# Attention then experts on one core: row numbers in their own tile, the experts' memory in another order, and the factor table made head pair by head pair

## The chip, the cores and the metric

The kernel runs on one core of one Trainium2 chip. The metric is the device time of one execution in microseconds (us). The engines are TensorE (PE; its weight loads are shown as PEld), VectorE (DVE), ScalarE (ACT), GpSimd (POOL) and the sync engine (SP), whose queue issues nearly all plain transfers. Each engine runs its own instructions in order; semaphores tie the engines to each other and to the transfers.

## What is computed

Two blocks in a row, all in float32. The first is attention with a sliding window and a bias that falls with distance; the second is a mixture of experts in which each token goes to the one expert that its logits choose, and none is dropped.

```python
# attention: batch 8, heads 8, sequence 576, head dim 64
scores = q @ k.T / sqrt(64)
rel    = pos[:, None] - pos[None, :]
slopes = 2.0 ** (-8.0 * (arange(8) + 1) / 8)            # one per head
scores = where((rel >= 0) & (rel < 128), scores - slopes * abs(rel), -1e9)
x      = softmax(scores) @ v                            # to (4608 tokens, 512)

# experts: 8 of them, hidden size 1024
logits = x @ w_gate                                     # (4608, 8)
e      = argmax(logits, axis=1)
gate   = softmax(logits)[e]
out[t] = gate[t] * (relu(x[t] @ w1[e[t]]) @ w2[e[t]])
```

## The kernel before

**Attention.** The work is cut into 32 units: 8 batches by 4 pairs of heads. A unit has four steps, written out by hand in one loop (`for u in range(NU + 1)`). `scores(u)` multiplies k by q on TensorE into four PSUM banks `sp` and takes the exponential on ScalarE into two tiles `e`. `factors(u, s)` multiplies `e` by a table `fac` on VectorE, L564 and L569. The table holds exp(-slope x distance) for each head, and zero outside the window, so bias and mask cost one product. `merge(u)` adds halves that belong to the same query on GpSimd, into `mg` (L576, L579). `values(u - 1, ...)` multiplies by v, and `totals(u - 1)` sums the weights with a matmul by a column of ones (L614), both on TensorE and one unit behind. The loads of q and k (`load_qk`, L534 and L535) run four units ahead, in a pool of five buffers.

**The table.** It is made once, ahead of the first unit. GpSimd writes a constant for each tile that is needed later (an identity, a triangle, counters, a row of zeros), then a matrix of distances `rel`. VectorE multiplies it by the eight slopes (L500), GpSimd cuts the window out with two selects over all heads (L501, L505), ScalarE takes the exponential over all heads (L509), and VectorE copies parts of it into the layout that the second half of a unit reads (L510 to L512). All of `scores(0)`'s exponentials stand behind L509 on ScalarE, and `factors(0, 0)` stands behind the copies, further small constants and `start_routing()` on VectorE.

**Routing.** As soon as a batch's attention is done, a list of tasks turns it into logits, chooses the expert, and sends each token's row to a DRAM buffer `x_rows`, sorted by expert, with an indirect transfer from GpSimd's queue (`scatter`, L178). A row is 514 words: 512 of x, then the token's number (as an integer), then its gate. The loop takes a few tasks from the list at two places in each unit (`do(n)`): none in the first seven units, and more in the last batch than in others. Eight transfers (`clear_rows`, L112) set `x_rows` to zero early on.

**The first two tiles of expert 0.** When all but the last two batches are routed, two tiles of 128 rows of expert 0 are complete. `early_group()` loads them, and `last_tasks()` does their transposes and layers among the tasks of the last batch. Their results are scaled by the gate into a tile `e` of attention's pool `ex`, and `send_out` (L416) sends each row to its place in the output, with an indirect transfer that takes its row numbers from an SBUF tile.

**The experts.** `experts(True)` runs 15 groups: the rest of expert 0 (two tiles), then by turns a small group x of one tile (rows that did not fit into an expert's 512) and a full expert of four tiles. A full expert uses a seven-product scheme in place of eight (`seven1`, `seven2`, matmuls at L880), a small group plain products (`layer1`, L450, and `layer2`, L458). At the head of each group's turn the kernel issues the *next* group's row load, `gather` (L981), into one of two buffers `xg`, then its w2. After the group's first layer comes w1 of the group after next, and the next group's rows are transposed on TensorE (`turn`, L441). Two facts about `xg` matter:

- Next to x it holds each row's token number and gate. ScalarE's scalings (L950, L462) read the gate; `send_out` reads the token number in place, through `ids_of_rows`. Only small groups copy theirs to a tile `si` first (`tokens`, with a mask that hides rows of others).
- With two buffers, the load issued during a small group goes into the buffer of the full expert just ahead of it, whose last sends have only just gone out.

**Memory.** Tile pools are stacked. Attention's pools close before the experts' open, so both start at the same base, and a tile of the experts has to wait for whatever attention kept at the same addresses. Attention opens, in this order and with these sizes per partition: `tab` (table, 17.0 KB), `ld` (q, k, v, 42.5 KB), `ex` (probs, e, mg, 31 KB), then the pools of x and routing. The experts' `moe_pools()` opens `weights1` (32 KB), `moe_sums` (32 KB), `moe_x` (the two `xg`, 16.1 KB), then two more. A second pool of weights, `weights0`, stays open throughout.

## Time and profile before

The median of three runs is 787.58 us (785.68 to 787.88); the profiled execution spans 785.5 us.

| engine | busy us | share of the span | instructions |
|---|---|---|---|
| TensorE, matmuls | 720.9 | 92% | 4646 |
| TensorE, weight loads | 585.1 | 74% | 4646 |
| VectorE | 367.8 | 47% | 618 |
| ScalarE | 225.8 | 29% | 535 |
| GpSimd | 175.1 | 22% | 186 |

Busy time of TensorE by stage, from the windows of the trace:

| stretch, us | what runs | TensorE busy | granted clock | GB/s of all transfers |
|---|---|---|---|---|
| 0 to 20 | table, first unit | 10.73 of 20 | 0.83 | 337 |
| 20 to 40 | units 2 to 5 | 17.91 of 20 | 1.00 | 325 |
| 120 to 200 | units with routing | 74.38 of 80 | 1.00 | 194 |
| 200 to 280 | last units, early group, first group | 68.59 of 80 | 0.91 | 104 |
| 350 to 380 | an expert, a small group, the next expert's rows | 27.12 of 30 | 0.94 | 198 |
| 380 to 400 | inside a full expert | 20.00 of 20 | 1.00 | 148 |

The trace puts an idle stretch of an engine down to whatever released the instruction after it: "PE tp L441 <- DMA xg<-x_rows" is time in which TensorE stood before a transpose at L441 until a row load had landed. A chain of waits follows the work that ended last back to the start, step by step. The granted clock is the share of TensorE's full speed that its throttle allowed in that stretch.

### The profile page before, as it was taken

What the parts mean: (1) busy time and instruction counts of PE and PEld (TensorE: products, weight loads), DVE (VectorE), ACT (ScalarE), POOL (GpSimd) and SP (SyncE); (2) the same over time, 40 slices, a digit from 0 to 9 for tenths busy, and PEclk for the clock granted to TensorE, in tenths of its full rate; (3) what the DMA queues carried; (4) which work ended last, traced back from release to release, by engine and by line L of the source; (5) the groups of instructions that cost most, each with busy time, mean ns of one, the idle gap of its engine ahead of it and who ended that gap; (6) DMA issues with size and microseconds to landing.
All of it is one profiled execution on the core that took longest, in us unless ns stands there. A gap on an engine that the chain in (4) does not pass through costs nothing.

```text
span 785.5 us, 11571 instructions
## 1 busy us (share of the span) xinstructions
PE 720.9 (92%) x4646; PEld 585.1 (74%) x4646; DVE 367.8 (47%) x618; ACT 225.8 (29%) x535; POOL 175.1 (22%) x186
## 2 busy tenths in 40 slices
PE   5899999999798799998999899899989989998992
PEld 4676777777583657887789688778968877896881
DVE  4567677776853022632543264254326335332620
ACT  3554465545421112222122121212212122121210
POOL 4537565776721010002001000200200020020001
PEclk8999899999999699999999999999999999999996
DMA  9996588762211738234830832483183247214001
GB/s 337 323 381 225 167 259 288 226 215 96 82 55 41 254 121 305 100 108 160 293 107 31 304 117 107 154 298 107 41 302 111 107 164 287 108 53 166 1 0 58
DMA packets 54286, 130.72 MB, mean 166 GB/s; under 512 B 4175, under 2 KB 4175, under 8 KB 54224
## 3 DMA queue, kind: packets, MB, share of 16 engines
q1 hardware_dynamic: 47696, 110.97, 41.0%
q0 software_dynamic: 6000, 18.92, 6.4%
q8 instruction: 38, 0.62, 0.3%
q14 instruction: 24, 0.20, 0.1%
q10 hardware_dynamic: 528, 0.02, 0.0%
HBM read 102.55 MB, written 28.12 MB: 166 GB/s over the span
## 4 chain that ended last, share of the span: by engine, by line
PE 67%; issue 13%; DVE 6%; DMA 5%; POOL 4%; ACT 3%; SPq 0%; POOLq 0%; DVEq 0%
PE b L880 16%; PE a L880 11%; PE c L880 11%; PE a L458 6%; PE sp L550 5%; PE m L595 5%; DMA xg<-x_rows 4%; PE sm L614 2%; PE m L693 1%; DMA out_dram<-zo,xg 1%; PE a L450 1%; PE m L450 1%; PE tp L441 1%; DVE probs L564 1%; PE b L450 1%
## 5 line engine op out<-in xcount | busy, mean ns | idle before, releaser
L416 POOL DMA_INDIRECT out_dram<-zo,xg x28 | 29.7, 1060 | 325.6 <-ACT zo L950 321.3
L550 PE MATMUL sp<-q_sb,k_sb 64*128 64x256 f32 (+2 forms) x640 | 72.0, 368 | 9.2 <-DMA k_sb<-in_kT_dram 5.2
L557 ACT ACTIVATE e<-sp 128x512 f32<-128x512 f32 x128 | 66.4, 601 | 47.3 <-PE sp L550 43.8
L550 PEld LDWEIGHTS sp<-q_sb,k_sb 64*128 64x128 f32 x640 | 63.5, 199 | 19.9 <-DMA q_sb<-in_qT_dram 5.1
L576 POOL TENSOR_TENSOR mg<-probs 128x768 f32<-128x768 f32 x31 | 57.4, 1850 | 74.0 <-DVE probs L569 30.0
L564 DVE TENSOR_TENSOR probs<-e,fac 128x1024 f32<-128x1024 f32 x32 | 46.8, 1463 | 46.3 <-ACT e L557 30.6
L595 PE MATMUL m<-probs,v_sb 128*64 128x256 f32 (+3 forms) x768 | 63.9, 315 | 2.3 <-DVE lgw L660 1.5
L595 PEld LDWEIGHTS m<-probs,v_sb 128*64 128x64 f32 x768 | 48.6, 138 | 18.9 <-issue 4.3
L458 PE MATMUL a<-w,h 128*128 128x512 f32 x128 | 56.9, 597 | 0.0
L950 ACT ACTIVATE zo<-zo,xg 128x256 f32<-128x256 f32 x42 | 19.1, 500 | 119.1 <-DVE zo L961 77.9
L880 PE MATMUL a<-xgT,w 128*128 128x256 f32 x224 | 53.0, 379 | 0.0
L880 PE MATMUL b<-xTs,w1s 128*128 128x256 f32 x224 | 52.9, 379 | 0.0
L880 PE MATMUL a<-w,h_sb 128*128 128x256 f32 x224 | 50.6, 379 | 0.0
L880 PE MATMUL b<-w2s,hs 128*128 128x256 f32 x224 | 50.6, 379 | 0.0
L880 PEld LDWEIGHTS a<-xgT,w 128*128 128x128 f32 x224 | 42.5, 190 | 8.7 <-issue 3.3
L178 POOL DMA_INDIRECT x_rows<-xs,slots x36 | 41.2, 1143 | 26.4 <-DVE xs L696 13.3
L880 PEld LDWEIGHTS b<-xTs,w1s 128*128 128x128 f32 x224 | 42.6, 190 | 5.8
L880 PEld LDWEIGHTS b<-w2s,hs 128*128 128x128 f32 x224 | 42.6, 190 | 5.8
L880 PEld LDWEIGHTS a<-w,h_sb 128*128 128x128 f32 x224 | 42.1, 190 | 5.5
L458 PEld LDWEIGHTS a<-w,h 128*128 128x128 f32 x128 | 24.2, 194 | 27.1 <-issue 27.1
L569 DVE TENSOR_TENSOR probs<-e,fac 128x1024 f32<-128x1024 f32 x32 | 41.2, 1288 | 0.0
L441 PE MATMUL tp<-ident,xg 128*128 128x128 f32 x92 | 16.4, 329 | 23.6 <-DMA xg<-x_rows 23.6
(211 smaller groups left out, 1164.6 us busy)
## 6 DMA issues: line engine op xcount, KB each, us to landing
w<-in_moe_w_dram SPq DMA_DIRECT2D x30, 2048.0 KB
q_sb<-in_qT_dram SPq DMA_DIRECT2D x32, 288.0 KB
k_sb<-in_kT_dram SPq DMA_DIRECT2D x32, 288.0 KB
x_rows<-zero_row SPq DMA_DIRECT2D x8, 1028.0 KB
xg<-x_rows SPq DMA_DIRECT2D x16, 514.0 KB
v_sb<-in_v_dram SPq DMA_DIRECT2D x8, 1024.0 KB
v_sb<-in_v_dram SPq DMA_DIRECT2D x8, 256.0 KB
xg<-x_rows SPq DMA_DIRECT2D x7, 257.0 KB
```

The lines of the kernel that those rows point to most:

```text
L178: ins = nc.gpsimd.indirect_dma_start(out=x_d[:, :], out_offset=bass.IndirectOffsetOnAxis(ap=slots[:, t : t + 1], axis=0), in_=row, in_offs ...
L416: ins = nc.gpsimd.indirect_dma_start(out=out[:, :], out_offset=bass.IndirectOffsetOnAxis(ap=g["ids"](g, j), axis=0), in_=row, in_offset=No ...
L441: nc.tensor.transpose(tp[:, db * P : (db + 1) * P], g["xg"][:, j, db * P : (db + 1) * P], ident[:])
L450: nc.tensor.matmul(ps[:, :n], lhsT=g["w1"][:, db, fb * P : (fb + 1) * P], rhs=g["xT"][:, db, :n], start=(db == 0), stop=(db == DB - 1),)
L458: nc.tensor.matmul(ps[:], lhsT=g["h"][:, fb, j * P : (j + 1) * P], rhs=g["w2"][:, fb, :], start=(fb == 0), stop=(fb == FB - 1),)
L550: nc.tensor.matmul(sps[s][par][:, c : c + n], lhsT=k_sb[u][half, k_lo[j] : k_lo[j] + P], rhs=q_sb[u][half, q0 : q0 + n], start=True, stop= ...
L557: nc.scalar.activation(exps[u][s][:, par, :], sps[s][par][:], AF.Exp, scale=D ** -0.5)
L564: nc.vector.tensor_tensor(to.rearrange("p a (j c) -> p a j c", c=2 * P), e.rearrange("p a (j c) -> p a j c", c=2 * P), fac[:, heads, None, ...
L569: nc.vector.tensor_tensor(to, e[:], fac2[:, heads, :], op=ALU.mult)
L576: eng.tensor_add(mg[:, :, : 3 * P].rearrange("p a (t c) -> p a t c", c=P), two[:, :, :, 0, :], two[:, :, :, 1, :],)
L595: nc.tensor.matmul(xp[par * HALF : (par + 1) * HALF, lo - q0 : hi - q0], lhsT=v_sb[b][:, j, h * D : (h + 1) * D], rhs=probs[u][:, par, c + ...
L880: nc.tensor.matmul(out_of[:, i, :], lhsT=lhs(i, k), rhs=rhs(k), start=(first and i == 0 and k == 0), stop=(k == nk - 1), skip_group_check= ...
```

## The change

It has four parts.

1. **Row numbers in their own tile.** Every group now copies its token numbers to a tile `si` of its own (two buffers, in the pool `plain`), by `tokens(g)`, with the mask for small groups and a plain copy for others. `send_out` reads them from there, so that a send no longer reads `xg`.
2. **The experts' memory by when attention lets go of it.** `weights1` opens after `moe_sums` and `moe_x`. The row buffers then lie where attention kept q, k and v, and the second pool of weights lies where it kept the last v and its probabilities.
3. **The table by head pair.** All distances and selects are made per pair of heads, ahead of everything else; constants that are needed later wait in a list `later`. Only the first pair's exponential and copies are done ahead of unit 0; `table(u + 1)` follows `factors` and `merge` of units 0 to 2. `start_routing()` moves behind unit 0.
4. **Pacing.** The last batch takes as many tasks per unit as the others do: at most one and two or three.

```diff
-    make_identity(nc, ident[:])
+    later = [lambda: make_identity(nc, ident[:])]
...
+    later.append(routing_constants)
...
-            out=out[:, :], out_offset=bass.IndirectOffsetOnAxis(ap=g["ids"](g, j), axis=0),
+            out=out[:, :], out_offset=bass.IndirectOffsetOnAxis(ap=g["si"][:, j : j + 1], axis=0),
...
-    def ids_of_rows(g, j):
-        return g["xg"].bitcast(I32)[:, j, Dm : Dm + 1]
-
-    def ids_masked(g, j):
-        return g["si"][:, j : j + 1]
+    def tokens(g):
+        bits = g["xg"].bitcast(I32)[:, : g["n"], Dm]
+        si = g["si"] = plain.tile([P, NJ], I32, name="si", bufs=2)[:, : g["n"]]
+        if "mask" in g:
+            nc.vector.tensor_tensor(si, bits, g["mask"][:, 0, :], op=ALU.bitwise_and)
+            nc.vector.tensor_tensor(si, si, g["mask"][:, 1, :], op=ALU.bitwise_or)
+        else:
+            nc.vector.tensor_copy(si, bits)
...
-        for h in range(H):
-            nc.vector.tensor_scalar_mul(fac[:, h, :], rel, 2.0 ** (-8.0 * (h + 1) / H))
-        nc.gpsimd.affine_select(
-            fac, fac, compare_op=ALU.is_ge, fill=MASKED,
-            base=0, pattern=[[0, H], [1, 2 * P]], channel_multiplier=-1,
-        )
...
-        nc.scalar.activation(fac, fac, AF.Exp, scale=-1.0)
-        nc.vector.tensor_copy(fac2[:, :, 2 * P : 3 * P + HALF], fac[:, :, : P + HALF])
-        nc.vector.tensor_copy(fac2[:, :, 3 * P + HALF :], fac[:, :, HALF:P])
+        def distances(hp):
+            pair = fac[:, 2 * hp : 2 * hp + 2, :]
+            for i in range(2):
+                nc.vector.tensor_scalar_mul(pair[:, i, :], rel, 2.0 ** (-8.0 * (2 * hp + i + 1) / H))
+            nc.gpsimd.affine_select(
+                pair, pair, compare_op=ALU.is_ge, fill=MASKED,
+                base=0, pattern=[[0, 2], [1, 2 * P]], channel_multiplier=-1,
+            )
...
+        def table(hp):
+            heads = slice(2 * hp, 2 * hp + 2)
+            nc.scalar.activation(fac[:, heads, :], fac[:, heads, :], AF.Exp, scale=-1.0)
+            nc.vector.tensor_copy(fac2[:, heads, 2 * P : 3 * P + HALF], fac[:, heads, : P + HALF])
+            nc.vector.tensor_copy(fac2[HALF:, heads, 3 * P + HALF :], fac[HALF:, heads, HALF:P])
+
+        for hp in range(HP):
+            distances(hp)
+        for make in later:
+            make()
+        table(0)
...
-        start_routing()
...
-            do(0 if slow else 1 if b < NB - 1 else 2)
+            do(0 if slow else 1)
             if u < NU:
                 factors(u, 1)
                 merge(u)
+                if u + 1 < HP:
+                    table(u + 1)
+                if u == 0:
+                    start_routing()
...
-            do(0 if slow else 2 if len(tasks) < 14 and b < NB - 1 else 3)
+            do(0 if slow else 2 if len(tasks) < 14 else 3)
...
-        w_pools[1] = st.enter_context(tc.tile_pool(name="weights1", bufs=1))
         pools["s"] = st.enter_context(tc.tile_pool(name="moe_sums", bufs=1))
         pools["x"] = st.enter_context(tc.tile_pool(name="moe_x", bufs=2))
+        w_pools[1] = st.enter_context(tc.tile_pool(name="weights1", bufs=1))
...
-            if "mask" in g:
-                tokens(g)
+            tokens(g)
```

## The prediction

> **What bounds the kernel now.** I read the page first, then who waits for whom on TensorE and on the queue of the sync engine (SP), then the chain of waits in three stretches, and last the busy time by windows.
>
> The page's first part: TensorE is busy for nine tenths of the span.
>
> ```profile
> PE 720.9 (92%) x4646; PEld 585.1 (74%) x4646; DVE 367.8 (47%) x618; ACT 225.8 (29%) x535; POOL 175.1 (22%) x186
> ```
>
> Of 785.5 us, 64.6 are left in which TensorE is idle. Some 20 us of these lie outside any reach (5.1 before the first q and k land, 15 after the last matmul at 770.2). So what counts is the other 44 us, and matmuls that ran slowly. TensorE's own list of waits names most of it:
>
> ```profile
> PE tp L441 <- DMA xg<-x_rows: 23.6, 8, 7.9
> PE sm L614 <- POOL mg L579: 6.2, 4, 2.1
> PE sp L550 <- DMA k_sb<-in_kT_dram: 5.2, 1, 5.2
> PE sp L550 <- ACT e L557: 4.1, 1, 4.1
> ```
>
> The row loads xg stand first: eight waits, 23.6 us. Why are they late? The same list for SP, which issues them:
>
> ```profile
> SPq L981 <- DMA out_dram<-zo,xg: 153.0, 7, 30.0
> SPq L981 <- DMA x_rows<-xs,slots: 40.4, 1, 40.4
> SPq L981 <- DMA out_dram<-e,xg: 16.3, 2, 9.5
> ```
>
> The loads wait for the sends of the *results*: a send reads its row numbers out of xg itself, so the buffer is held until the send has landed. The chain of waits over one hand-over from an expert to the small group after it (355 to 374 us; start, length, what):
>
> ```profile
> 360.05 0.91 ACT zo L950 x2
> 362.30 2.73 DMA out_dram<-zo,xg
> 365.66 4.62 DMA xg<-x_rows
> ```
>
> ScalarE reads xg for the last time at 360.96; the send lands at 365.03; the loads go out at 365.24. TensorE has finished the small group's first layer at 366.43 and waits 2.56 us, to 368.99. The six hand-overs after full experts wait 2.56, 2.55, 2.42, 2.49, 2.32 and 2.64 = 15.0 us; the one after the first group 0.72; the one at the end of attention 7.93. Together 23.6.
>
> The chain at the end of attention:
>
> ```profile
> 252.60 2.72 DMA out_dram<-e,xg
> 255.58 3.81 DMA xg<-x_rows
> 259.53 1.95 PE tp L441 x8
> 262.41 3.75 PE a L450 x8
> ```
>
> The scatters that this load needs had landed at 238.9 (the 40.4 us wait ended there). It then stood 16.3 us more, for the two early sends out of a tile e, whose memory the xg buffer takes over. And TensorE comes back slow: 3.75 us for eight matmuls that take 1.89 later.
>
> The chain at the start:
>
> ```profile
> 6.31 1.96 POOL fac L501
> 8.32 1.96 POOL fac L505
> 10.30 1.92 ACT fac L509
> 12.24 0.96 DVE fac L510
> 17.77 2.88 POOL mg L576
> 20.64 1.41 POOL mg L579
> ```
>
> The first scores are done at 8.65, but ScalarE can't turn to them before 12.11, and VectorE's first product waits for copies until 15.34. Unit 2's scores start at 22.76; from there a unit takes 4.55 us, all of it TensorE.
>
> **What the Trainium skill says.** "TensorE: Matmul & The Clock Gate", Part 1 (what's actually happening): about 3.4 us of idling halves the clock, about 3.4 us of work restores it, in windows that run freely. The trace agrees in kind: the first hand-over below (eight transposes after 2.55 us of idling) is slow, the second isn't, so it depends on where the window lies.
>
> ```profile
> 438.26 1.97 PE L441 MATMUL tp<-ident,xg 128*128 128x128 f32 x8 [2.55 <-DMA xg<-x_rows]
> 507.05 1.09 PE L441 MATMUL tp<-ident,xg 128*128 128x128 f32 x8 [2.42 <-DMA xg<-x_rows]
> ```
>
> "DMA: Bandwidth & Descriptors", anatomy of one DMA: about 2 us of a DMA are fixed, mostly the receipt of its last byte. The send's 2.73 us fits; no queue order makes it shorter, so the gain must come from not waiting for it. "SBUF — State Buffer", who interferes with whom: a VectorE instruction with two SBUF inputs contends with GpSimd's reads. The trace agrees: mg took 2.88 us beside such products, 1.81 alone.
>
> **The change part by part.**
>
> *Row numbers in a tile si.* VectorE copies them once per group (a new copy of 2 or 4 integers; the nearest row, the masking of si, takes 0.15 us; nine copies, 1.4 us in all). For a full expert the copy stands behind the hidden sums and before a wait for TensorE of 3 to 4 us: hidden. The copy waits only for xg, and for the sends of the si two groups back, long landed. In exchange xg is free when ScalarE's last scaling ends: the load goes out at 361.1 in place of 365.24. The first part needs 3.75 us (365.24 to 368.99): 364.9. The second landed 4.62 after its issue at 365.66: 4.1 earlier, 366.2, when it is wanted after 367.5. Both are before their use, so the wait is gone whole: 15.0 us for six. The queue of SP then holds w2, which waits for TensorE's end of that expert (359.3), and w1, which waits for the small group's first layer: neither comes ahead of the rows. The slow clock goes too. From tp's start to the next layer's first matmul took 3.16, 3.42, 2.33, 3.40, 2.37 and 3.33 us; at 2.33 each, 4.0 less. I take 3.0 of these, as a cold window may fall elsewhere: **-18.0** (15 to 19.5). The first hand-over, held by a plain send: **-0.7**.
>
> *Memory.* Attention's pools stack as table 17.0 KB per partition, q/k/v to 59.5 KB, probs/e/mg to 90.5 KB. Before, the experts' order weights 32 KB, sums 32, xg 16.1 lays xg at 64 to 80 KB, over probs and e. After, sums, xg, weights: xg lies at 32 to 48 KB, over q/k/v, read for the last time at 217; the weights over the rest of these and e. So the first load waits for the scatters alone: out at 239, landed at 242.8; layer two of the early group ends on TensorE at 251.6. Gone: 7.93 of waiting, and the slow clock: tp 1.94 against 1.09, layer one 3.75 and 2.68 against 1.89 = 3.5. Against it 0.7, ScalarE's copy behind its scaling to 252.33. **-10.7** (8 to 11.4). The new wait: w1 of the first small group is held by the early sends, to 255.3. It was issued at 257.28 before, so it isn't later. Behind it on SP stand the small group's rows and w2. At 2 MB by the 380 GB/s of the start, 5.5 us, plus 2, w1 lands by 263 and the rows by 265; they are wanted at 252.3 + 1.0 + 13.9 = 267, w1 at 281. Hidden by some 2 us; the least certain margin here.
>
> *Table and start.* GpSimd begins with the distances: index and cast end near 1.6 (0.33 and 0.40, from 0.8), VectorE's eight products of 0.21 near 3.3. The two selects of 1.95 become four pairs of pieces of 1.95 / 4 = 0.49: pair 0 done near 3.2, all near 6.4; the constants (2.9 us of GpSimd before the index, 0.8 to 3.7) come after, to about 10. ScalarE's table load is 1.28; a pair's exponential is 512 wide, 0.6 like an e: done by 4.5. VectorE's copies and memsets, 3.1 us in all, shrink to about 2.2 and begin at 4.5: done by 7. So TensorE's scores, from 5.15, are now what is waited for: half done at 6.9, e from 7.0 to 9.7, products 9.8 to 11.0. Unit 1's q and k: at about 385 GB/s, 2.49 MB of queue ahead of and with them land near 9.3; scores(1) 9.3 to 12.5 (cold clock 13.5); values(0) to 14.6 (16.5); mg(0) from 11.0, 2.3 alone or 4.3 beside VectorE, to 13.3 or 15.3; totals; scores(2) between 15.2 and 17.5 in place of 22.76. Middle 16.3: **-6.5** (5 to 7.5). Three later exponentials (0.6) and six copies (about 0.3) fall in units 1 to 3, where ScalarE has 2.9 and VectorE 2.4 of 4.55 us: hidden.
>
> Do the loads follow? The windows:
>
> ```profile
> 60.00:65.00 5.00, 5.00 (x62) 3.85 (x58) 4.79 (x9) 2.86 (x6) 1.55 (x3) 1.00 0.96 347
> 65.00:70.00 5.00, 5.00 (x60) 3.49 (x60) 2.72 (x3) 3.13 (x7) 4.60 (x5) 1.00 0.41 119
> ```
>
> (busy PE, PEld, DVE, ACT, POOL; granted clock, DMA share, GB/s.) The transfers run without a pause to 65 us. Added up in queue order with the zeroing of rows: unit 5's q and k are complete at 6.16 MB, near 18.5, wanted at 29; unit 9's at 12.7 MB, near 36, wanted at 52. The margin holds.
>
> *Pacing.* Two or three tasks per unit in the last batch become at most one and two. In the new order unit 30's mg stands ahead of three scatters on GpSimd instead of behind them, which cost 2.02 us (part of the 6.2); a 1.48 us wait for the gate's product may go or move. **-2** (0 to -3).
>
> Sum: 18.0 + 0.7 + 10.7 + 6.5 + 2.0 = 37.9; 787.6 - 37.9 = 749.7.
>
> **Rivals.**
> - *Start bound by transfers* (0.08): DMA share is 1.0 from 2.5 us on. If units 1 and 2 wait for q and k, or the constants hold up mg(0), some 5.5 of the 6.5 are lost: 755. Against: unit 2's loads are at 3.08 MB, near 11.
> - *The rows stay late* (0.07): two 514 KB halves beside w2 and the last sends; a new releaser takes the place of the send, all six waits remain and only the rest comes: 787.6 - 19.9 = 768. Against: 1.5 us of slack, and the first load has little traffic beside it.
> - *Slower* (0.03): the pieces of the table enter the path of units 1 to 3 (3 x 0.9 = 2.7), the nine copies too (1.4), and a small group's rows behind the held w1 cost as much as the load before saved, so that nothing is gained: 787.6 + 4.1 = 792. For it: SP works in order. Against: ScalarE and VectorE have room, and the held load leaves earlier than before.
>
> **How the numbers follow.** The likeliest case, 0.82, is 749.7. With all lower bounds it is 787.6 - 28.7 = 759, with all upper ones 787.6 - 42.3 = 745. Both at once are unlikely; 744 to 758 holds some 0.75 of the first case and nearly all of the second: 0.8. Faster by over 0.3%: 0.96; within: 0.01; slower: 0.03.
>
> **What would show it.** Right: TensorE's waits for xg fall from 23.6 us to under 2; SP's waits at the row loads name ScalarE in place of sends; the transposes at the end of attention follow the last early matmul within 1 us; unit 2's scores begin near 16. Wrong: a new wait before these transposes, a wait for q or k in the first units, a transpose of the first small group behind its rows, or a half clock in places where it was full.

## The result, and the profile after

The changed kernel takes 748.10 us (median of four, 747.69 to 748.83) beside 786.80 us before (785.68 to 787.88): ratio 0.9509, 95% interval 0.9491 to 0.9528. The profiled executions span 785.5 and 747.0 us, and the traces' 38.5 us are what is accounted for below. The forecast was 749.7.

First part of the page, changed kernel:

```profile
PE 706.0 (95%) x4646; PEld 573.1 (77%) x4646; DVE 371.0 (50%) x633; ACT 226.1 (30%) x538; POOL 175.7 (24%) x192
```

The number of matmuls is the same, yet TensorE is busy 14.9 us less: the same matmuls ran faster, at a granted clock of 0.990 in place of 0.966. The other 23.6 us are waits.

TensorE's list of waits, changed kernel (us in all, times, longest):

```profile
PE sm L635 <- POOL mg L600: 7.8, 4, 3.5
PE a L450 <- DMA xg<-x_rows: 3.8, 5, 1.7
PE a L459 <- DVE si L439: 0.9, 1, 0.9
PE tp L450 <- ACT e L471: 0.8, 1, 0.8
```

The 23.6 us before the first transposes (tp) are gone. Four things are new: 3.8 us for the *second* half of an expert's rows (a), a wait of 0.8 us at the end of attention, a wait of 3.5 us for a merge, at the start, and, inside the first line of the list, one of 1.87 us for the merge of unit 28, at 190.78 us, about where the kernel before waited 1.48 us for the gate's product. The 0.9 us before L459 isn't new: before, the same 0.94 us stood there, with VectorE's `xT` (L443) as the releaser.

The same list for the queue of SP:

```profile
SPq L1006 <- ACT h L463: 138.5, 6, 23.1
SPq L1006 <- ACT zx L471: 67.4, 7, 14.5
```

The row loads (L1006) no longer stand behind sends of results but behind ScalarE, as forecast. (At the head of the list stands L463, which doesn't read xg. In the first hand-over the scaling ahead of it, L975, which does, ends at 340.93, and the load goes out at 340.95.) The early sends now hold a load of weights instead (L199, 11.7 us in two waits).

Reading the same points of both timelines gives the account:

| point | before, us | after, us | gained by then | in this stretch |
|---|---|---|---|---|
| unit 2's scores | 22.76 | 18.44 | 4.3 | 4.3 |
| unit 13's scores | 90.48 | 81.66 | 8.8 | 4.5 |
| unit 28's scores | 186.67 | 178.95 | 7.7 | -1.1 |
| early group's second layer | 237.70 | 227.87 | 9.8 | 2.1 |
| first group's second layer | 279.26 | 260.59 | 18.7 | 8.8 |
| first small group's rows turned | 301.02 | 281.47 | 19.6 | 0.9 |
| end | 785.5 | 747.0 | 38.5 | 19.0 |

**The hand-overs.** The timeline of SP, GpSimd and TensorE in the first one, changed kernel (start, length, what, and the idle time before it):

```profile
340.80 1.16 POOL L422 DMA_INDIRECT out_dram<-zo,si  x1 [1.01 <-ACT zo L975]
340.95 1.72 SPq L1006 DMA_DIRECT2D xg<-x_rows  x2
342.27 0.97 POOL L422 DMA_INDIRECT out_dram<-zo,si  x1 [0.30 <-ACT h L463]
342.77 0.48 SPq L205 DMA_DIRECT2D w<-in_moe_w_dram  x1
346.24 1.04 PE L450 MATMUL tp<-ident,xg 128*128 128x128 f32 x8
349.02 0.63 PE L450 MATMUL a<-ident,xg 128*128 128x128 f32 x4 [1.75 <-DMA xg<-x_rows]
```

The load goes out as the last send does, not after it has landed. The first half is there when TensorE asks for it (no wait at tp). The second isn't; the chain of waits has it:

```profile
341.38 7.50 DMA xg<-x_rows
...
407.86 6.18 DMA xg<-x_rows
```

7.50 us here and 6.18 in the next hand-over, where the load of before took 4.62.

**The end of attention**, TensorE's timeline, changed kernel:

```profile
242.54 1.09 PE L450 MATMUL tp<-ident,xg 128*128 128x128 f32 x8 [0.78 <-ACT e L471]
244.58 3.64 PE L459 MATMUL a<-xT,w 128*128 128x256 f32 x8 [0.94 <-DVE si L439]
248.01 1.94 PE L459 MATMUL b<-xT,w 128*128 128x256 f32 x8
```

The wait of 7.93 us has become 0.78, but the first eight matmuls still take 3.64 us.

**The start**, GpSimd and TensorE, changed kernel:

```profile
8.68 1.01 POOL L75 TENSOR_SCALAR_AFFINE_SELECT lt_strict<-lt_strict 128x128 f32<-128x128 f32 x1
10.26 1.02 POOL L92 CAST first_w<-first_w_i 128x8 f32<-128x8 int32 x1
12.34 1.20 POOL L92 CAST kx<-kx_i 128x32 f32<-128x32 int32 x1
13.68 0.98 POOL L92 CAST tail<-tail_i 128x4 f32<-128x4 int32 x1
15.51 1.80 POOL L597 TENSOR_TENSOR mg<-probs 128x768 f32<-128x768 f32 x1
17.77 0.73 PE L635 MATMUL sm<-mg,one_c 128*32 128x320 f32 x8 [3.49 <-POOL mg L600]
```

The constants run from 7.86 to 15.55, in place of 2.9 us. Four of them take about a microsecond each beside VectorE's products (casts of the same kind take 0.19 and 0.21 between them); before, these four took 0.18 to 0.28 each. That is 3.4 of the 4.8 us more; the rest was not followed. Unit 0's products are done at 11.23; the merge starts at 15.51.

### The profile page after: what moved, and what is told of

Same layout as the page of the kernel before. It is cut to its first block, busy times and chain, and to the rows that moved or that the text cites. A ratio compares the mean times of both kernels' runs of the same rounds, so it can differ in the third digit from the quotient of the medians.

```text
span 747.0 us, 11609 instructions
## 1 busy us (share of the span) xinstructions
PE 706.0 (95%) x4646; PEld 573.1 (77%) x4646; DVE 371.0 (50%) x633; ACT 226.1 (30%) x538; POOL 175.7 (24%) x192
## 4 chain that ended last, share of the span: by engine, by line
PE 70%; issue 11%; DVE 6%; POOL 5%; DMA 4%; ACT 2%; SPq 0%; POOLq 0%; DVEq 0%
PE b L905 17%; PE a L905 11%; PE c L905 11%; PE a L467 6%; PE sp L571 4%; PE m L616 4%; DMA xg<-x_rows 4%; PE m L459 2%; PE sp L467 2%; PE a L459 2%; PE sm L635 2%; PE m L714 2%; POOL x_rows L184 2%; PE b L459 2%; PE c L459 1%
## 5 line engine op out<-in xcount | busy, mean ns | idle before, releaser
L422 POOL DMA_INDIRECT out_dram<-zo,si x28 | 29.5, 1053 | 325.7 <-ACT zo L975 321.4
L571 PE MATMUL sp<-q_sb,k_sb 64*128 64x256 f32 (+2 forms) x640 | 68.3, 356 | 6.1 <-DMA k_sb<-in_kT_dram 5.0
L571 PEld LDWEIGHTS sp<-q_sb,k_sb 64*128 64x128 f32 x640 | 60.4, 191 | 16.3 <-DMA q_sb<-in_qT_dram 5.0
L585 DVE TENSOR_TENSOR probs<-e,fac 128x1024 f32<-128x1024 f32 x32 | 45.0, 1406 | 42.1 <-ACT e L578 31.3
L975 ACT ACTIVATE zo<-zo,xg 128x256 f32<-128x256 f32 x42 | 19.1, 500 | 119.4 <-DVE zo L986 78.2
L905 PEld LDWEIGHTS a<-w,h_sb 128*128 128x128 f32 x224 | 42.1, 190 | 5.5
L590 DVE TENSOR_TENSOR probs<-e,fac 128x1024 f32<-128x1024 f32 x32 | 39.6, 1239 | 0.5 <-ACT e L578 0.5
L422 POOL DMA_INDIRECT out_dram<-zx,si x9 | 9.4, 1045 | 126.8 <-ACT zx L471 126.8
```

What stands on the lines that cost most here:

```text
L422: ins = nc.gpsimd.indirect_dma_start(out=out[:, :], out_offset=bass.IndirectOffsetOnAxis(ap=g["si"][:, j : j + 1], axis=0), in_=row, in_of ...
L571: nc.tensor.matmul(sps[s][par][:, c : c + n], lhsT=k_sb[u][half, k_lo[j] : k_lo[j] + P], rhs=q_sb[u][half, q0 : q0 + n], start=True, stop= ...
L585: nc.vector.tensor_tensor(to.rearrange("p a (j c) -> p a j c", c=2 * P), e.rearrange("p a (j c) -> p a j c", c=2 * P), fac[:, heads, None, ...
L590: nc.vector.tensor_tensor(to, e[:], fac2[:, heads, :], op=ALU.mult)
L905: nc.tensor.matmul(out_of[:, i, :], lhsT=lhs(i, k), rhs=rhs(k), start=(first and i == 0 and k == 0), stop=(k == nk - 1), skip_group_check= ...
L975: nc.scalar.activation(o[:, th, dh, i, :], src[:, i, :], AF.Copy, scale=g["xg"][:, j, Dm + 1 :])
```

## The experiments

Each kernel is the changed one with the edit shown, except the sixth, which starts from the kernel before. The ratio is to the kernel before on the same chip.

| run | median, us | range | ratio to before (95%) | span of the trace |
|---|---|---|---|---|
| no_si | 769.02 | 764.94 to 769.81 | 0.9748 (0.9704 to 0.9791) | 767.7 |
| no_layout | 758.25 | 758.02 to 759.71 | 0.9627 (0.9593 to 0.9661) | 757.8 |
| no_table | 755.25 | 753.95 to 756.94 | 0.9585 (0.9550 to 0.9620) | 755.1 |
| no_pacing | 748.80 | 748.53 to 749.16 | 0.9510 (0.9476 to 0.9543) | 746.7 |
| consts_later | 748.91 | 748.43 to 751.30 | 0.9526 (0.9489 to 0.9563) | 747.5 |
| before_clear_early | 786.66 | 785.45 to 789.67 | 1.0003 (0.9990 to 1.0017) | 785.0 |
| w2_later | 750.14 | 749.95 to 752.68 | 0.9546 (0.9510 to 0.9582) | 748.1 |
| early_turn | 745.75 | 744.54 to 746.28 | 0.9476 (0.9442 to 0.9509) | 744.2 |
| gates_too | 742.28 | 741.80 to 745.69 | 0.9444 (0.9407 to 0.9482) | 740.1 |
| both_gates | 741.80 | 740.05 to 743.60 | 0.9421 (0.9385 to 0.9457) | 740.8 |
| three | 741.81 | 740.21 to 743.68 | 0.9425 (0.9390 to 0.9460) | 740.1 |
| best | 735.93 | 735.23 to 736.93 | 0.9345 (0.9327 to 0.9363) | 734.6 |

The runs lie on several chips, and beside them the kernel before took 786.4 to 788.6 us (medians). So a difference to the changed kernel's 748.10 us is uncertain by some 2 us. By the ratios no_si stands 18.8 us above it and not 20.9, no_layout 9.3 and not 10.2, and gates_too 5.1 below it and not 5.8.

### One part undone at a time

**Row numbers read out of xg again (no_si).**

```diff
-            out_offset=bass.IndirectOffsetOnAxis(ap=g["si"][:, j : j + 1], axis=0)
+            # groups without a mask: g["xg"].bitcast(I32)[:, j, Dm : Dm + 1]
```

> The changed kernel, but full experts and the two plain groups read their row numbers out of xg again, as before; the memory order, the table and the pacing stay. Theory (the sends held the row buffers): the six hand-overs cost 18.0 to 19.0 us more and the first small group's 0.7, so 748.1 + 19.2 = 767; TensorE waits for xg in front of the transposes again, six times about 2.5 us, and the queue of the sync engine names sends at the row loads. Rival (the rows come early because of where xg lies in memory, whatever holds the numbers): no change within 2 us, 748 to 750.

769.0, 20.9 more than the changed kernel. TensorE's waits and SP's:

```profile
PE tp L454 <- DMA xg<-x_rows: 15.7, 7, 2.6
```

```profile
SPq L1010 <- DMA out_dram<-zo,xg: 179.5, 8, 30.0
```

The seven waits and their cause are back. The memory order was left as changed, so it isn't what freed these loads; the rival falls. Of the 20.7 us between the two traces, 1.3 were lost ahead of the first group's second layer (261.89 against 260.59), where TensorE waits for no rows in either; the other 19.4 are close to the 19.2 of the theory.

**The second pool of weights first again (no_layout).**

```diff
+        w_pools[1] = st.enter_context(tc.tile_pool(name="weights1", bufs=1))
         pools["s"] = ...
         pools["x"] = ...
-        w_pools[1] = st.enter_context(tc.tile_pool(name="weights1", bufs=1))
```

> The changed kernel, but the second pool of weights opens first again, so that xg lies over the probabilities and e. Theory: the load at the end of attention waits for the early sends again; a wait of about 8 us in front of the first transposes, 748.1 + 8.8 = 757 (755 to 759). Rival (the end of attention gained because the last batch's tasks are done earlier, not by the memory order): 748 to 751.

758.3, 10.2 more. TensorE's timeline:

```profile
252.17 1.94 PE L450 MATMUL tp<-ident,xg 128*128 128x128 f32 x8 [7.91 <-DMA xg<-x_rows]
255.05 3.75 PE L459 MATMUL a<-xT,w 128*128 128x256 f32 x8 [0.94 <-DVE si L439]
```

The wait of before is back, to 0.02 us. From the early group's second layer (230.37 against 227.87) to the first group's (271.48 against 260.59) it costs 8.4 us. The other 2.5 us were lost *before* that, most of them in units 29 and 30, whose instructions this edit doesn't touch (see the last table of this section).

**Table, constants and the routing's start ahead of unit 0 again (no_table).**

```diff
-        for hp in range(HP): distances(hp)
-        for make in later: make()
-        table(0)
+        for make in later: make()          # ahead of rel; then all heads at once, as before
...
-                if u + 1 < HP: table(u + 1)
-                if u == 0: start_routing()
```

> The changed kernel, but constants, the whole table and the routing's start stand ahead of unit 0 as before. If the table is worth only the start of the kernel: unit 2's scores begin near 22.8 us in place of 18.4, 748.1 + 4.3 = 752.4. If the earlier start also keeps the first scatters out of the way of the products in units 11 to 13 (where 4.5 us more were gained): TensorE falls to half its clock there, and the time is near 757.

755.3, 7.2 more: between the two, nearer the second. Unit 2's scores begin at 23.80, 5.4 later than in the changed kernel, and unit 13's at 92.02, 10.4 later. So units 2 to 13 cost another 5.0 here, as in the kernel before. The windows show where (busy PE, PEld, DVE, ACT, POOL with their instructions; granted clock, DMA share, GB/s). Before:

```profile
80.00:85.00 5.00, 4.53 (x24) 3.94 (x24) 3.13 (x8) 1.82 (x6) 2.34 (x3) 0.50 0.01 3
85.00:90.00 5.00, 5.00 (x55) 3.80 (x52) 3.34 (x6) 2.67 (x6) 1.56 (x1) 0.84 0.52 132
```

The changed kernel:

```profile
80.00:85.00 5.00, 5.00 (x55) 4.15 (x51) 3.70 (x9) 3.03 (x8) 4.14 (x5) 1.00 0.87 275
85.00:90.00 5.00, 5.00 (x64) 3.94 (x62) 1.84 (x3) 3.03 (x8) 4.22 (x5) 1.00 0.91 331
```

The changed kernel with this edit:

```profile
80.00:85.00 5.00, 3.43 (x17) 2.84 (x18) 3.95 (x12) 2.15 (x13) 2.35 (x3) 0.67 0.01 3
85.00:90.00 5.00, 5.00 (x44) 3.82 (x44) 3.29 (x5) 2.31 (x5) 0.37 (x1) 0.65 0.36 118
```

A stretch at half clock of some 5 us, which the changed kernel doesn't have, comes with the later start. A merge and a product meet there, as in the kernel before (shown at before_clear_early): they begin 0.10 us apart, and the product takes 3.03 us. Some of the 10.4 us was gained back later: the end is 8.1 apart.

**Two or three tasks per unit in the last batch again (no_pacing).**

```diff
-            do(0 if slow else 1)
+            do(0 if slow else 1 if b < NB - 1 else 2)
...
-            do(0 if slow else 2 if len(tasks) < 14 else 3)
+            do(0 if slow else 2 if len(tasks) < 14 and b < NB - 1 else 3)
```

> The changed kernel, but the last batch takes two or three tasks per unit again. Theory: merges stand behind scatters on GpSimd in the last batch, a wait of about 2 us in unit 31 is back: 748.1 + 2 = 750 (749 to 751). Rival (the last batch has enough room for the tasks either way): 748.1 within 0.5.

748.8, 0.7 more; the ratios can't be told apart (0.9510 against 0.9509). TensorE's timeline, at two places:

```profile
206.82 0.73 PE L635 MATMUL sm<-mg,one_c 128*32 128x320 f32 x8 [2.02 <-POOL mg L600]
...
246.84 1.97 PE L459 MATMUL a<-xT,w 128*128 128x256 f32 x8 [0.94 <-DVE si L439]
```

The wait of 2.02 us is back and the early group's second layer begins 2.26 later (230.13), just as the theory says. But the first group's first layer, behind the very same waits of 0.78 and 0.94, runs at full clock (1.97 against 3.64), and by that group's second layer (261.17 against 260.59) only 0.6 is left. The pacing was worth its 2 us, and in these two traces the clock took them.

The pacing also moved a wait. With the old one TensorE waits 1.48 us for the gate's product at 191 us, as in the kernel before, and not for unit 28's merge. With the new one TensorE comes to that merge's sums with fewer tasks done and waits 1.87 us. (The merge stands behind scatters in both; it begins at 188.39 us in the changed kernel and at 187.47 here.) Behind this new wait the clock is halved in most of the other kernels (last part of this section).

### What held the start, and what was gained in units 11 to 13

**Constants behind the merges (consts_later).**

```diff
-        for make in later: make()
         table(0)
...
+                if u < 6:      # after merge(u): the row of zeros first, then the others a few at a time
+                    for make in (later[-2:], later[:1], later[1:2], later[2:6], later[6:10], later[10:-2])[u]: make()
+                if u == 6: start_routing()
```

> The changed kernel, but GpSimd's constants no longer stand between the distances and the first merge: they are made a few at a time behind the merges of units 0 to 5, and the routing's start behind unit 6. Theory (the constants, 7.7 us of GpSimd, held up the first merge and so unit 2): TensorE's wait of 3.5 us for the first mg falls below 1.5, unit 2's scores begin near 16.3 in place of 18.4, 748.1 - 2 = 746. Rival (the first merge is late because of VectorE's products or the transfers): no change, or later if the pieces lengthen the merges of units 1 to 5.

GpSimd and TensorE:

```profile
12.99 1.85 POOL L595 TENSOR_TENSOR mg<-probs 128x768 f32<-128x768 f32 x1 [2.51 <-DVE probs L588]
...
16.72 2.06 PE L569 MATMUL sp<-q_sb,k_sb 64*128 64x256 f32 x20
```

The merge follows its product, and unit 2 begins at 16.72, 1.7 sooner than in the changed kernel's trace: so the constants did hold it there. (This is near the 16.3 of the forecast.) In the traces of the other kernels that keep the changed start, unit 2 begins at 17.53 to 18.89, so the gain is 0.8 to 2.2 us. One of these, best, shows a second limit. GpSimd and TensorE there:

```profile
12.27 0.21 POOL L92 CAST kx<-kx_i 128x32 f32<-128x32 int32 x1
13.49 1.80 POOL L599 TENSOR_TENSOR mg<-probs 128x768 f32<-128x768 f32 x1
```

```profile
11.78 3.89 PE L573 MATMUL sp<-q_sb,k_sb 64*128 64x256 f32 x20 [2.97 <-DMA k_sb<-in_kT_dram]
```

The constants stand where they stand in the changed kernel, but unit 1's products come later and miss the last two casts; the merge starts at 13.49 in place of 15.51. Yet unit 2 begins at 18.89, since unit 1's scores waited 2.97 us for k and then ran at half clock. Of the ten later kernels with the pieced table, eight show such a wait, of 1.27 to 2.97 us; the changed kernel's trace doesn't. So the transfers are the next limit at the start, close behind the constants.

But consts_later isn't faster: 748.9. Half a microsecond went in unit 4, while GpSimd makes constants, and another in units 5 to 12; 0.7 us survive to unit 28 and are gone by unit 31 (199.61 against 199.41), behind a half clock at 190 us. Later this run avoids the half clock at 245 and meets one at 345 instead.

**Zeroing sooner, in the kernel before (before_clear_early).**

```diff
-                if 0 < u <= E:
-                    clear_rows(u - 1)
+                if 0 < u <= E // 2:
+                    clear_rows(2 * u - 2)
+                    clear_rows(2 * u - 1)
```

> The kernel before, but the eight transfers that zero the row buffer are issued two per unit in units 1 to 4 in place of one per unit in 1 to 8; nothing else. Theory (in the kernel before, the first scatters waited for the zeroing, which ended at 65 us with all other transfers, and ran into the merges and products of units 10 to 13): the first scatter no longer waits, TensorE stays at full clock there, and 4 to 5 us are gained: ratio to before 0.995. Rival (the scatters were late because of the routing's own chain): no change, 787; a third case: q and k of units 5 to 9 come late behind the zeroing and it is slower.

786.7, no change. The theory falls in its main point: the last zeroing is issued at 33.9 instead of 48.6 us, and the first scatter goes out at 64.33 instead of 65.23, still after 2.8 us of idling. But this 0.9 has an effect. GpSimd and VectorE, before:

```profile
74.29 1.84 POOL L576 TENSOR_TENSOR mg<-probs 128x768 f32<-128x768 f32 x1
74.33 2.89 DVE L564 TENSOR_TENSOR probs<-e,fac 128x1024 f32<-128x1024 f32 x1 [1.46 <-ACT e L557]
```

and in this run:

```profile
72.85 1.83 POOL L576 TENSOR_TENSOR mg<-probs 128x768 f32<-128x768 f32 x1
74.33 1.44 DVE L564 TENSOR_TENSOR probs<-e,fac 128x1024 f32<-128x1024 f32 x1 [1.46 <-ACT e L557]
```

Before, a merge and a product begin 0.04 us apart, and the product takes 2.89 us; here the merge has a head start of 1.5 and the product takes 1.44. The gate's product behind it comes 1.45 sooner, and unit 13 begins at 87.87 instead of 90.48: 2.6 gained, more than the 1.45, with less of the half clock. So the collision is part of the cause of what was lost there. In the changed kernel that merge stands at 67.03 and the product at 70.01, apart, and takes 1.23. By the end these 2.6 us are gone again, too: spans 785.0 and 785.5. Of them, 1.6 went near 210 us, at a half clock behind a wait of 2.02 us for a merge; the kernel before has the same wait there, and full clock behind it.

### What is left at the hand-overs

**w2 behind w1 during a small group (w2_later).**

```diff
                 gather(after[0])
-                after[0]["w2"] = load_w2(...)
+                if g["n"] == NJ: after[0]["w2"] = load_w2(...)   # small groups: behind get_w1(after[1])
```

> The changed kernel, but during a small group the next expert's w2 is issued behind the w1 of the group after, not right behind the expert's rows. Theory (w2 and the second half of the rows share the transfer engines): the second halves land in time, TensorE's wait for xg (3.8 us in five places) goes, 748.1 - 3 = 745 to 746. Rival (the last two sends of the expert ahead, which are under way beside the rows, delay them): the waits remain, 748.

750.1, 2.0 more, which the intervals of the two ratios don't separate. TensorE's timeline in the first hand-over, and VectorE's list of waits:

```profile
349.32 0.63 PE L450 MATMUL a<-ident,xg 128*128 128x128 f32 x4 [0.61 <-DMA xg<-x_rows]
```

```profile
DVE w2s L874 <- DMA w<-in_moe_w_dram: 6.1, 5, 2.3
```

The first wait fell from 1.75 to 0.61; five others are 0.34 to 0.57, so all six sum to 3.1 in place of 3.8. But four other kernels that leave w2 and these loads as they are (no_pacing, no_layout, no_table, consts_later) have first waits of 0.59 to 1.94 us and sums of 3.3 to 4.6, so this run doesn't show that w2 has a share. The theory falls: most of the wait stays. And w2 is needed early: VectorE makes sums of w2 among the products of the next first layer, now waits 6.1 us for it, and TensorE waits 1.4 us for VectorE. (The traces end 1.1 us apart; 0.7 of that lies ahead of the first small group, 282.20 against 281.47, where half clock came in near 75 and 190 us.) That the sends delay the second halves was not isolated.

**Gates out of xg as well (gates_too).**

```diff
+        gates = g["gates"] = plain.tile([P, NJ], F32, name="gates", bufs=2)[:, : g["n"]]
+        nc.vector.tensor_copy(gates, g["xg"][:, : g["n"], Dm + 1])
...
-                nc.scalar.activation(..., AF.Copy, scale=g["xg"][:, j, Dm + 1 :])
+                nc.scalar.activation(..., AF.Copy, scale=g["gates"][:, j : j + 1])
```

> The changed kernel, and each group's gates are copied out of xg as well, next to its row numbers, so that ScalarE's scalings no longer read xg. Theory (the second half of an expert's rows lands late because the load still waits for ScalarE's last scaling): the load goes out near the end of the expert's first layer, some 20 us sooner, and TensorE's five waits for xg (3.8 us) go: 748.1 - 3.8 = 744.3. Rival (something else on the sync engine's queue holds these loads as long): the waits remain and the nine small copies cost nothing, 748.

742.3, 5.8 less than the changed kernel. The timelines of SP and TensorE:

```profile
316.39 1.02 SPq L1008 DMA_DIRECT2D xg<-x_rows  x2
...
344.55 1.04 PE L452 MATMUL tp<-ident,xg 128*128 128x128 f32 x8
345.42 0.60 PE L452 MATMUL a<-ident,xg 128*128 128x128 f32 x4
```

The load goes out at 316.39 instead of 340.95, and neither half is waited for; no wait for xg is left in TensorE's list. From the moment TensorE is ready for the first transpose to the first matmul of the small group's second layer, the six hand-overs take 33.0 us in all before (15.0 of waiting and 18.0 more), 15.7 in the changed kernel and 10.5 here (1.75 each). The remaining reader of xg was what held it, and the rival falls. Of the 6.9 us between the two traces these 5.2 are the edit's. The other 1.7 were gained before: behind the same waits of 0.78 and 0.94 us the first group's first layer ran at full clock here (1.97 us for the eight matmuls that took 3.64).

### The end of attention

**The first group's rows earlier (early_turn).** The early group's buffer is reused as soon as its transposes are done.

```diff
+            # after the last scatter; the early group's gates were copied out
+            first = early["next"] = dict(n=EJ, e=0, apart=True, xg=plain.tile([P, EJ, RW], F32, name="xg2"))
+            nc.sync.dma_start(first["xg"][:], x_d[EJ * P : CAP, :]...)
             for j in range(EJ):
+                if j == 1:
+                    for i in range(EJ): turn(first, [i], full())
                 layer2(g, j, full(), ...)
```

> The changed kernel, but the first group's rows are loaded into the early group's own buffer as soon as its transposes are done (its gates are copied out first), and are transposed between the two halves of the early group's second layer. Theory (the two short waits at the end of attention, 0.78 and 0.94 us, and the half clock behind them, 1.75 us, all come from transposing at that place): 748.1 - 3.4 = 744.7. Rival (the half clock belongs to that stretch of time and not to these waits): the two waits go, 1.7 us, 746.4.

745.8, 2.4 less. TensorE:

```profile
235.25 1.04 PE L450 MATMUL sp<-ident,xg 128*128 128x128 f32 x8
...
243.94 1.99 PE L459 MATMUL a<-xT,w 128*128 128x256 f32 x8 [0.78 <-ACT e L471]
```

From the early group's second layer to the third piece of the next first layer it now takes 19.1 us in place of 21.9: 2.8 less, 0.94 of it the second wait and 1.65 the half clock. The wait for ScalarE stays, at another instruction. Whether the half clock "comes from these waits" isn't settled by this run, since no_pacing and gates_too had both and ran at full clock.

**Both (both_gates)**, without a second copy of the gates:

> The changed kernel with the gates copied out and the first group's rows loaded early and transposed between the halves of the early group's second layer. The two gains are at different places, so they should add: the waits for xg and 0.9 us of waits at the end of attention go, 748.1 - 3.8 - 2.4 = 742 (half clock at other places may give or take 3).

741.8: the sum that was expected, but gates_too alone already stood half a microsecond above it (their ranges overlap), so the two gains did not add as far as these runs show. Beside gates_too it gains only 1.1 us at the end of attention, as the half clock that early_turn saved there had not come in gates_too either. TensorE's timeline shows what it lost:

```profile
191.03 1.22 PE L637 MATMUL sm<-mg,one_c 128*32 128x320 f32 x8 [1.87 <-POOL mg L602]
...
194.09 3.83 PE L573 MATMUL sp<-q_sb,k_sb 64*128 64x256 f32 x19
```

In gates_too the same place has a wait of 1.80 and then full clock (2.00 us for these 19 matmuls). Unit 31 begins 2.7 us later for it.

**And the constants behind the merges (three)**, the edit of consts_later on top:

> The same as the run before it, with GpSimd's constants behind the merges of units 0 to 5 as well. If a gain at the start only shifts the work against the places where TensorE's clock is halved, as it did when the constants were moved alone: within 2 us of the run before it, either way. If it adds: 742 - 1.7 = 740.

741.8, the same. Unit 2 begins at 15.88, the soonest of all, 2.8 us sooner than in both_gates, and nothing of it is seen at the end, for the second time.

**Two merges on VectorE (best).** The wait of 1.87 is for the merge of unit 28, that stands behind scatters on GpSimd's queue; so is one of 1.21 for unit 24.

```diff
-            eng = nc.vector if u == NU - 1 else nc.gpsimd
+            eng = nc.vector if u in (NU - 8, NU - 4, NU - 1) else nc.gpsimd   # on top of both_gates
```

> The changed kernel with the gates copied out, the first group's rows turned early, and the merges of units 24 and 28 on VectorE, which stands idle there, in place of GpSimd, where they stand behind scatters. In the run with the first two of these, TensorE waited 1.2 and 1.9 us for these two merges, and its clock was halved right after the second, which cost another 3. Theory (the half clock near 190 us follows from that wait): the two waits and that half clock go, 741.8 - 3.1 - 3 = 736. Rival (half clock comes somewhere in every run, whatever is removed): only the waits go and some of it comes back at another place, 739 to 742.

735.9: 12.2 less than the changed kernel. TensorE's list of waits:

```profile
PE sm L637 <- POOL mg L602: 1.2, 1, 1.2
PE a L461 <- ACT e L473: 0.8, 1, 0.8
```

Both waits are gone and so is the half clock near 190; in this trace none came elsewhere before TensorE's last matmul. "Half clock comes somewhere in every run" falls, as it does with no_pacing. But only one execution was traced: this one's mean clock is 0.993, and the other four had 0.989 to 0.992, so some of them may have had a stretch of it. The size of the gain also depends on what it is compared with. By unit 31, both_gates with its half clock is 6.2 us behind, and gates_too, which waits 1.80 us for the same merge and keeps full clock, 3.5.

### Where the clock was halved

Windows of 5 us over each whole trace, up to TensorE's last matmul, that were granted less than 0.9:

| kernel | starts of these windows, us |
|---|---|
| before | 10, 15, 80, 85, 250, 255, 260, 265, 370, 435, 440, 575, 710 |
| changed | 245 |
| before_clear_early | 10, 15, 80, 210, 215, 250, 255, 260, 265, 370, 435, 440, 505, 710 |
| no_si | 75, 190, 195, 350, 420, 555, 690, 695 |
| no_layout | 190, 195, 250, 255 |
| no_table | 80, 85, 200 |
| no_pacing | none |
| consts_later | 190, 345, 350 |
| w2_later | 75, 190, 195 |
| early_turn | 75, 190 |
| gates_too | 75 |
| both_gates, three | 190, 195 |
| best | none |

Near 75 and 190 us, kernels with the same work on TensorE up to there differ. no_layout against the changed kernel, at 190 us, no_layout first:

```profile
190.00:195.00 5.00, 4.05 (x22) 2.29 (x24) 1.28 (x7) 0.00 (x0) 3.20 (x5) 0.60 0.37 105
```

```profile
190.00:195.00 5.00, 4.22 (x40) 3.22 (x40) 2.58 (x11) 0.63 (x5) 3.03 (x5) 1.00 0.34 105
```

Both waited 1.87 us for the same merge; one did 22 matmuls in this window and the other 40. Ten traces have this wait, of 1.80 to 1.87 us: the next 19 matmuls of unit 30's scores take 2.00 us in two of them (the changed kernel and gates_too) and 2.81 to 3.83 in eight. "TensorE: Matmul & The Clock Gate" in the Trainium skill, Part 1, says that the clock's windows run freely, so that a transition varies with the phase. The traces agree in that the same wait is followed by half clock in one run and not in another; that the phase is what differs, they don't show. Near 75 us it is the same: a wait of 1.37 us is followed by 20 matmuls in 3.30 us in gates_too, and one of 1.38 by 20 in 2.06 in consts_later. So a trace shows where a halving is *possible* (here after waits of 1.4 us and more, and once after 0.78 and 0.94 us close together), and a difference of 2 to 5 us at such a place says little of the edit.

## Why the prediction was right, and where it wasn't

The total was right to 0.6 us in the spans (37.9 forecast, 38.5 found), and that it came so near is luck. The end of attention brought 1.9 us less than forecast and the start 2.2 less; 3.4 that nobody had forecast came in units 11 to 28, and 1.0 more at the hand-overs. (The upper ends of the parts add up to 42.1 and not to 42.3, without effect.) Of the four signs of being right two came, SP's waits at ScalarE and the prompt transposes at the end of attention. The waits for xg are 3.8 us and not under 2, and unit 2 begins at 18.44 and not near 16.

| step | forecast | found | |
|---|---|---|---|
| six hand-overs | -18.0 | -19.0 | right in size; one claim in it wrong |
| first small group's rows | -0.7 | -0.9 | right |
| end of attention | -10.7 | -8.8 | wait right, clock mis-sized |
| start | -6.5 | -4.3 | constants mis-sized |
| pacing | -2 | -2.1 | right there; later taken by the clock |
| units 11 to 13 | none | -4.5 | missed |
| units 13 to 28 | none | +1.1 | missed |

**Hand-overs.** "The loads go out at 361.1 in place of 365.24" held in kind: they go out when ScalarE has ended, and no_si shows that the sends were the cause. The 15.0 us before the first transposes are gone. What failed is "The second landed 4.62 after its issue ... Both are before their use": that took the length of a load which had gone out *after* the sends had landed and used it for one that goes out beside the last two of them and ahead of w2. It takes 6.2 to 7.5 us (which of the two lengthens it stays open), and 3.8 us of waits remain. The forecast had seen this as a rival ("two 514 KB halves beside w2 and the last sends"), but for all or nothing. Against that, "I take 3.0 of these" for the slow clock was too little: the transposes took 18.0 us from the first of them to the next layer, and take 15.7 with the 3.8 of new waits, so 11.9 without; 6.1 are gone. The clean time of 2.33 each, from which the forecast reckoned, still had a wait of 0.33 in it; gates_too shows 1.75. So -15.0 - 6.1 + 3.8 = -17.3 lie here; the other 1.7 are around them (0.6 in the second layer after the first hand-over, 0.5 in the transposes after the first group) and were not followed further.

**End of attention.** 7.93 became 0.78, as forecast to 0.1, and no_layout brings it back by the memory order alone. The failing step is "and the slow clock: ... = 3.5". Only 1.7 came (tp 0.85, layer one 0.11 and 0.74); the first eight matmuls stayed slow behind 0.78 + 0.94 us of idling. The forecast took the half clock to be the price of the long wait. The size of a wait doesn't decide it: 2.42 us of idling at 507.05 before were followed by full clock, these 1.7 by half. w1's margin ("the least certain") held: no wait for it.

**Start.** The step that failed is "the constants ... come after, to about 10": they were priced at their time alone, 2.9 us, and took 7.7 beside VectorE's products, although the same paragraph gave mg two prices for exactly this reason. "SBUF — State Buffer" in the Trainium skill (who interferes with whom), which it cited, was applied to one GpSimd instruction and not to its neighbours. consts_later finds the missing 1.7 and shows that it is worth nothing at the end. The rival "start bound by transfers", whose case included that the constants hold up mg(0), was right on that cause; it cost 2.2 and not 5.5. Its other half, unit 1 waiting for k, isn't in the changed kernel's trace but in eight of the later ones.

**What was missed.** The forecast followed each edit to its first effect. It did not ask what a start some 4 us sooner does in the routing: there a merge and a product met within 0.04 us before and don't now, and a stretch of 5 us at half clock is gone as well. no_table (both back with the late start) and before_clear_early (2.6 of the 4.5 us gained when the product is no longer stretched) show both ends. It saw that the 1.48 us wait for the gate's product "may go or move", but not that 1.87 us before unit 28's merge would take its place. What held the first scatter in the kernel before for 2.8 us, with zeroing out of the way, stays open.

Of the rivals that end elsewhere, "slower" had nothing for it: the row copies (nine, 1.4 us of VectorE in all) and the pieces of the table cost no wait of TensorE that the changed kernel's trace shows (the 0.94 us put down to si at L439 stood there before, too).

## What to carry to other kernels

- A buffer is free when its *last* reader is done, so list them all. The change took one small reader (the sends' row numbers) out of a large buffer and won 19 us; taking out the next one (the gates, one small copy per group) moved the load from 5 to 28 us ahead of its use and won 5 more.
- Before pricing a transfer or a small instruction by a row of the old trace, ask what ran beside it there and what will now: 4.6 us for the second half of a load became 6.2 to 7.5, casts of 0.2 us became 1.0 to 1.2.
- On a kernel bound by TensorE, remove the waits that stand ahead of a possible halving of the clock, even short ones, before moving the start. Two merges on an idle engine brought 6 us beside a kernel that had the half clock, of which only 3 were waits; 1.7 and 2.8 us won at the start brought nothing that could be seen at the end.

## What was not expected of the hardware

- Waits of 1.4 to 1.9 us, and once of 0.78 and 0.94 close together, were followed by half clock for the next 2 to 5 us. The Trainium skill ("TensorE: Matmul & The Clock Gate", Part 1) gives about 3.4 us of idling; here the measurement decides, and it says that less can do, though not each time (eight times of ten behind 1.80 to 1.87 us).
- A GpSimd cast of 8 numbers per partition took 1.02 us beside a VectorE product of two tiles and 0.19 between products, while the filling of a counter, which reads no tile, took 0.13 beside one (at 13.49 us in the changed kernel); a product took 2.89 us when a GpSimd merge had started 0.04 us ahead of it, and 1.44 when it had started 1.5 us ahead.
